# Equal tile sizes for the strided attention cells, and a new planner of the issue order

## The chip, the cores and the metric

The kernel runs on one core of a Trainium2 chip. A core has five engines that run their own instruction streams: TensorE (PE, matrix products; PEld is its weight load), VectorE (DVE), ScalarE (ACT), GpSimdE (POOL) and SyncE (SP, which here issues every DMA). Matmuls read SBUF and write PSUM, which has eight banks of 2 KB per partition. The metric is the device time of one execution, in microseconds.

## The reference

Three stages follow each other. Only the first has masks:

```python
scores = (1 / sqrt(64)) * q @ k.T               # 4 batches, 8 heads, 576 tokens, head size 64
mask_local   = (rel >= 0) & (rel < 32)           # heads 0..3, rel = query - key
mask_strided = (rel >= 0) & (key % 32 == query % 32)   # heads 4..7
attn = softmax(where(mask, scores, -1e9)); x = attn @ v          # x: 2304 tokens x 512
h = x @ w_in; solu = h * softmax(h)                              # 512 -> 1024
y = layernorm(solu) * g_ln @ w_out                               # 1024 -> 512
out = (y @ w_a * (y @ w_b)) @ w_out2                             # 512 -> 1536 -> 512
```

Weights arrive as 64-bit floats, and are rebuilt as 32-bit floats on the chip.

## The kernel before

**Attention.** A strided head has 32 residues of 18 tokens each, and tokens see only their own residue. The kernel puts three residues in a cell of 54 queries by 54 keys; a head's 16 residues of one parity make five such cells and one of a single residue, 18 by 18. A strided tile is one pair of heads and one parity j: 12 cells, of which ten are 54 wide and two are 18 wide. There are 16 strided tiles (4 batches, 2 pairs, 2 parities). A local cell has 64 queries and 96 keys; a local tile has eight cells (one tile in three has two), and there are 24.

For each tile PE runs two operations of the plan. `scores` (L705 to L710) first adds the mask to PSUM by a product of an identity in bf16 with a table of 0 and a large negative number (L706), and then adds q times k per cell (L709; fp32, each cell shows as two records in the trace). `pv` multiplies the transposed softmax with v: L803 in fp32 for batch 0, and L808, L809, L810 for the others, three fp16 products per cell that add up. `pv` of all tiles writes one PSUM bank, `xbank`, head 0 to partitions 0 to 63 and head 1 to 64 to 127. An operand of up to 32 rows or columns uses a 32-wide part of the PE array, one of 33 to 64 a 64-wide part.

**After attention.** `moe1` computes h (L861, 24 matmuls per 128 tokens), its softmax and layer norm on DVE, ACT and POOL, and transposes the result by DMA; `s2` computes y (L910). L910 needs all of w_out: eight raw pieces are loaded, rebuilt (ACT L468, DVE L470, L475, L481), measured (ACT L514), scaled, and split into two fp16 parts (ACT L546, DVE L548, eight times each). The last stage runs products of y with w_a and w_b (L1288) and then with w_out2 (L1353).

**The order.** Every operation goes through `Plan.op` with an engine, a cost in microseconds, and for PE a number of columns. `Plan.schedule` makes a forward list schedule by keys, a backward one that gives new keys, adds noise (a seeded random number), and repeats 120 times; the order with the shortest replay is emitted. The replay doubles the cost of a PE operation when the columns of the time window before it were below `ENTRY`; `forward` also prefers operations with many columns per microsecond (`dense`) when few columns were issued lately. So the order on all engines and DMA queues follows from the costs given to `Plan.op`. One instruction stream per engine runs in this order: an instruction that waits holds back all that stand behind it on its engine.

Of the kernel before, what the change touches and what calls it, by code (L numbers as in the profile page):

```python
# [25 lines left out]
ST = 32  # L26
# [7 lines left out]
NM = S // QT  # L34
# [16 lines left out]
NEG = -(2.0 ** 120)  # L51
PASSES = ((0, 0), (0, 1), (1, 0))

PARAM = dict(back=12, first=40, early=(0,), seed=4, noise=0.1, direct=(0,), span=4.0, dense=1500, cols=5000, pf1=(),
             pf2=(), ph1=(), pv=(), pp=(8,), ps1=(), ps2=(), passes=120, e=3,
             PT=3, raw=2, rawl=2, raws=2, qkT=2, V=2, wk=2, xt=1, ln=2, lnT=2, ys=2, raw64=3, f64f=4, att=100.0,
             win=24.5, wout=128.6, moff=-69.7, moe=96.6, conv2=257.2, dconv=15.0, p2=385.0, pre=6.5, fine=(),
             lat=1, plo=(0,), sooner=0.0, soon=(((0, 0), (0, 1), (1, 0), (1, 1)), ((0, 2), (0, 3), (1, 2), (1, 3), (2, 0), (2, 1), (2, 2), (2, 3)), ()), cv=-40.0, dcv=10.0)
# [37 lines left out]
class Plan:  # L96
# [3 lines left out]
    TICK, ENTRY = 10.24 / 3, 3060  # L100
    SAME = dict(DVE=0.13, ACT=0.15, POOL=0.05, PE=0.0, CTL=0.0)
    ENGINES = ("PE", "DVE", "ACT", "POOL", "SP", "CTL")

    def __init__(self):
        self.ops, self.writer, self.readers, self.key, self.sooner, self.shift = [], {}, {}, 0.0, 0.0, 0.0

    def op(self, eng, us, fn, r=(), w=(), nbytes=0, after=()):
        o = Op()
        o.eng, o.us, o.fn, o.key, o.nbytes, o.sooner = eng, us, fn, self.key - self.sooner, nbytes, self.sooner
        o.deps, o.starts, o.outs = set(after), set(), []  # L110
# [25 lines left out]
        o.deps.discard(o)  # L136
        self.ops.append(o)
        return o

    def latency(self, a, b):  # L140
        if a.eng == b.eng and a.eng != "SP":
            return self.SAME[a.eng]
        return PARAM["lat"] * (0.28 if a.eng == "PE" else 0.14)

    def schedule(self):

        order, self.shift = self.forward(), 0.0
        best, keys = self.length(order), [o.key for o in self.ops]  # L150
        rnd = random.Random(PARAM["seed"])
        for n in range(PARAM["passes"]):
            if n % PARAM["back"] == 0 and n >= PARAM["first"]:
                for o, key in zip(self.ops, keys):
                    o.key = key
                self.shift = shift
                self.forward()
            self.backward()
            for o in self.ops:
                o.key += rnd.gauss(0.0, PARAM["noise"]) - o.sooner  # L160
            self.shift = self.TICK * (n % 4) / 4
            order = self.forward()
            length = self.length(order)
            if length < best:
                best, keys, shift = length, [o.key for o in self.ops], self.shift
        for o, key in zip(self.ops, keys):
            o.key = key
        self.shift = shift
        order = self.forward()
        self.mean = best  # L170
        return order

    def length(self, order):
        return sum(self.replay(order, self.TICK * (n + 0.5) / 4) for n in range(4)) / 4

    def replay(self, order, shift):
        free = {e: 0.0 for e in self.ENGINES}
        dma = hw = 0.0
        count, start, end = collections.defaultdict(float), {}, {}
        for o in order:  # L180
            e = o.eng
            at = free[e]
            for d in o.deps:
                at = max(at, end[d] + self.latency(d, o))
            for d in o.starts:
                at = max(at, start[d])
            us = o.us
            if e == "PE":
                if count[int((at + shift) / self.TICK) - 1] < self.ENTRY:
                    us *= 2  # L190
                self.fill(count, at + shift, us, o.nbytes)
            start[o] = at
            free[e] = end[o] = at + us
            if e == "SP":
                hw = max(hw, at) + 0.55
                dma = max(dma, hw + 0.65) + o.nbytes / 250e3
                free[e] = max(free[e], hw, dma - 2.0)
                end[o] = dma + 0.75
        return max(end.values())

    def fill(self, count, t, us, cols):
        end = t + us
        while t < end:
            n = int(t / self.TICK)
            e = min(end, (n + 1) * self.TICK + 1e-4)
            count[n] += cols * (e - t) / us
            t = e

    def backward(self):
        for o in self.ops:  # L210
            o.n, o.ready = len(o.outs), 0.0
        free = {e: 0.0 for e in self.ENGINES}
        ready = {e: [o for o in self.ops if o.eng == e and not o.n] for e in self.ENGINES}
        dma = 0.0
        for _ in self.ops:
            at, e = min((max(free[e], min(o.ready for o in ready[e])), e) for e in self.ENGINES if ready[e])
            o = max((o for o in ready[e] if o.ready <= at), key=lambda o: (o.end, o.seq))
            ready[e].remove(o)
            end = free[e] = at + o.took
            if e == "SP":  # L220
# [4 lines left out]
            for d in o.deps:  # L225
                d.ready = max(d.ready, end + self.latency(d, o))
                d.n -= 1
                if not d.n:
                    ready[d.eng].append(d)
# [1223 lines left out]
```

## Time and profile before

| | |
|---|---|
| median of 3 runs | 740.57 us (739.69 to 744.24) |
| profiled execution: span | 742.1 us |
| PE busy | 719.9 us, 97% |
| DVE busy | 519.3 us, 70% |
| ACT busy | 432.2 us, 58% |
| POOL busy | 117.2 us, 16% |
| chain that ended last | 88% PE, 6% DVE, 2% ACT, 2% DMA |

The profiled execution's own time is not listed apart from the runs; its span of 742.1 us stands 1.5 us above their median. Busy PE time counts a matmul from its start to its modelled end, so matmuls that overlap count once, and a PE that is slow in issuing still counts as busy. The distance from one matmul's start to the next one's tells more than its length. The column PEclk is the share of PE's full clock that was granted: 1.00 is 2.4 GHz and 0.50 is 1.2 GHz.

### The profile page before, as it was taken

How to read it: one execution, taken by the hardware profiler on the slowest of the kernel's cores; microseconds unless marked ns; L12 is line 12 of the kernel's file. 1: busy time of each engine (PE TensorE's matmuls, PEld its weight loads, DVE VectorE, ACT ScalarE, POOL GpSimd, SP SyncE). 2: the span in 40 equal slices, each digit the busy share in tenths (PEclk: the TensorE clock that was granted, in tenths of full speed). 3: DMA queues.
4: the chain of work that ended last, by engine and by line, in shares of the span. 5: the costliest groups of instructions: out<-in, count | busy, mean ns of one | idle time of the engine just before them, and what ended most of it. 6: DMA issues, size and time to landing. Idle time of an engine off the chain costs nothing.

```text
span 742.1 us, 14124 instructions
## 1 busy us (share of the span) xinstructions
PE 719.9 (97%) x5444; PEld 479.2 (65%) x5444; DVE 519.3 (70%) x1020; ACT 432.2 (58%) x824; POOL 117.2 (16%) x194
## 2 busy tenths in 40 slices
PE   6989889999999999999999999999999999999997
PEld 4867668888787888878655555555555546555553
DVE  4888987858776864898899998547868454434252
ACT  4667977676777876785768666544454333132230
POOL 4441435412433432210000000000000000000000
PEclk9988979999999999999999999999999999999999
DMA  9788996976998585567537034406705031711304
GB/s 212 181 193 222 193 153 136 221 178 160 218 208 165 118 190 141 149 123 254 194 142 272 20 129 129 142 28 187 246 1 170 29 126 44 236 57 46 124 6 165
DMA packets 159327, 109.61 MB, mean 148 GB/s; under 512 B 103702, under 2 KB 137500, under 8 KB 159260
## 3 DMA queue, kind: packets, MB, share of 16 engines
q1 hardware_dynamic: 159260, 108.71, 56.6%
q8 instruction: 43, 0.70, 0.4%
q14 instruction: 24, 0.20, 0.1%
HBM read 65.42 MB, written 27.53 MB: 125 GB/s over the span
## 4 chain that ended last, share of the span: by engine, by line
PE 88%; DVE 6%; ACT 2%; DMA 2%; issue 1%; SPq 0%; POOL 0%; POOLq 0%; DVEq 0%
PE M L1288 31%; PE o L1353 19%; PE y L910 12%; PE h L861 12%; PE s L709 4%; PE s L624 3%; PE xbank L808 2%; PE xbank L803 1%; PE s L706 1%; DMA raw<-in_moe_w_b_dram 1%; PE xbank L810 1%; DMA rawk<-in_k_dram 1%; DMA rawq<-in_q_dram 1%; PE xbank L809 1%; ACT qkT L632 1%
## 5 line engine op out<-in xcount | busy, mean ns | idle before, releaser
L1288 PE MATMUL M<-y,w 128*128 128x384 f16 x1512 | 256.4, 326 | 0.9 <-DVE y L1235 0.6
L1288 PEld LDWEIGHTS <-w 128*128 128x128 f16 x1512 | 147.8, 98 | 102.5 <-issue 1.6
L1353 PE MATMUL o<-wo,p 128*128 128x512 f16 x648 | 147.9, 379 | 0.0
L1353 PEld LDWEIGHTS <-p 128*128 128x128 f16 x648 | 63.3, 98 | 71.0
L910 PE MATMUL y<-lnT,wout 128*128 128x256 f16 x864 | 105.0, 279 | 0.8 <-ACT ys L913 0.6
L910 PEld LDWEIGHTS <-wout 128*128 128x128 f16 x864 | 83.9, 100 | 15.4 <-issue 2.5
L861 PE MATMUL h<-win,xh 128*128 128x512 f32 x288 | 81.5, 422 | 1.4 <-DVE wk L869 1.3
L1295 ACT COPY M<-M 128x384 f32<-128x384 f32 x72 | 33.5, 466 | 68.3 <-PE M L1288 68.2
L861 PEld LDWEIGHTS h<-win,xh 128*128 128x128 f32 x288 | 55.1, 201 | 13.2 <-DVE wk L869 1.1
L1338 ACT ACTIVATE p<-A 128x384 f16<-128x384 f32 x72 | 36.7, 520 | 33.2 <-DVE A L1337 33.1
L1360 DVE SCALAR_TENSOR_TENSOR ob<-o,osc,op 128x512 f32<-128x512 f32 x36 | 27.0, 750 | 40.4 <-PE o L1353 35.1
L1340 DVE SCALAR_TENSOR_TENSOR p<-A,p 128x384 f16<-128x384 f32 x72 | 38.8, 552 | 8.0 <-ACT p L1338 7.7
L709 PE MATMUL s<-qkT 64*54 64x54 f32 (+2 forms) x672 | 38.4, 254 | 2.7 <-ACT qkT L632 2.4
L1299 DVE TENSOR_TENSOR A<-M,V 128x384 f32<-128x384 f32 x36 | 20.0, 555 | 30.0 <-PE M L1288 29.9
L475 DVE SCALAR_TENSOR_TENSOR f64f<-f64f,raw 128x512 int32<-128x512 int32 x52 | 39.4, 762 | 1.4 <-ACT f64f L468 0.7
L866 DVE TENSOR_REDUCE st<-h 128x1 f32<-128x1024 f32 x18 | 22.0, 1221 | 25.9 <-PE h L861 25.9
L861 PE MATMUL h<-win,xl 128*128 128x512 f32 x144 | 40.0, 400 | 0.0
L1337 DVE TENSOR_TENSOR A<-A,M 128x384 f32<-128x384 f32 x36 | 19.9, 552 | 27.0 <-PE M L1288 26.8
L468 ACT ACTIVATE f64f<-raw 128x512 f32<-128x512 f32 x52 | 34.5, 670 | 7.1 <-DMA raw<-in_moe_w_out_dram 2.9
L1310 ACT COPY V<-M 128x384 f32<-128x384 f32 x36 | 17.1, 475 | 34.4 <-PE M L1288 34.3
L709 PEld LDWEIGHTS s<-qkT 64*54 64x54 f32 (+2 forms) x672 | 27.7, 143 | 13.4 <-issue 3.6
L784 POOL TENSOR_TENSOR e<-e,r 128x324 f32<-128x324 f32 (+2 forms) x30 | 26.6, 889 | 59.5 <-DVE r L740 59.5
(170 smaller groups left out, 1135.7 us busy)
## 6 DMA issues: line engine op xcount, KB each, us to landing
raw<-in_moe_w_out_dram SPq DMA_DIRECT2D x20, 512.0 KB
o_scr<-ob SPq DMA_DIRECT2D x36, 256.0 KB
op<-o_scr SPq DMA_DIRECT2D x36, 256.0 KB
raw<-in_moe_w_a_dram SPq DMA_DIRECT2D x12, 512.0 KB
raw<-in_moe_w_b_dram SPq DMA_DIRECT2D x12, 512.0 KB
y_scr<-y SPq DMA_DIRECT2D x14, 384.0 KB
y<-y_scr SPq DMA_DIRECT2D x14, 384.0 KB
y_scr<-ys SPq DMA_DIRECT2D x18, 256.0 KB
```

The source lines that it names most:

```text
L468: act(0.67, lambda: nc.scalar.activation(f(), raw()[:, :, 1].bitcast(F32), AF.Copy, scale=2.0 ** -112), (raw,), (f,))
L475: nc.vector.scalar_tensor_tensor(fi, fi, 3, raw()[:, :, 0], op0=ALU.logical_shift_left, op1=ALU.bitwise_or)
L709: nc.tensor.matmul(s[64 * half:64 * half + nq, f, col:col + kk], g.T()[w, 0, q0:q0 + nq], g.T()[w, 1, k0:k0 + kk], start=False, stop=n == ...
L784: pool(0.1 + 1.2 * pl, lambda: nc.gpsimd.tensor_tensor(ev(), ev(), r()[:, :ng].unsqueeze(2).to_broadcast([128, ng, nk]), op=ALU.mult), (r, ...
L861: nc.tensor.matmul(h()[:, 512 * n:512 * n + 512], xs[xa]()[:, kk], win[wa][:, kk, 512 * n:512 * n + 512], start=(pi == 0 and kk == 0), sto ...
L910: nc.tensor.matmul(y()[:, 256 * mi:256 * mi + 256], wout[:, kk, wa, 128 * m:128 * m + 128], lnT()[:, xa, kk], start=(pi == 0 and kk == 0), ...
L1288: nc.tensor.matmul(bank()[:, :HB], w()[:, wa, a, kk], y7[b]()[:, xa, kk], start=first and pi == 0 and kk == 0, stop=pi == 2 and kk == 1, s ...
L1295: act(TA, lambda: nc.scalar.copy(dst()[:, :HB], src()[:, :HB]), (src,), (dst,))
L1338: act(TA, lambda x=x, v=v: nc.scalar.activation(v(0), x(), AF.Copy, scale=2.0 ** -PEXP), (x,), ((pu, 0, c, t),))
L1340: dve(TD, lambda x=x, v=v: nc.vector.scalar_tensor_tensor(v(1), x(), 2.0 ** -PEXP, v(0), op0=ALU.mult, op1=ALU.subtract), (x, (pu, 0, c, t ...
L1353: nc.tensor.matmul(o(), pus[u]()[:, xa, c, 128 * tt:128 * tt + 128], wo()[:, 2 * u + c, wa], start=(u == 0 and c == 0 and pi == 0), stop=( ...
L1360: dve(0.75, lambda: nc.vector.scalar_tensor_tensor(ob(), o(), osc()[:, tt:tt + 1], op(), op0=ALU.mult, op1=ALU.add), (o, osc, op), (ob,))
```

## The change

The kernel computes the same. Six things differ.

1. In `scores` a cell of 18 queries is computed with 36 (`LEAST`): 18 further rows of the output that nobody reads. It then needs a 64-wide part of the array, as the cells of 54 do.
2. The mask product is split: instead of one product with the whole array, one per 64 output partitions, in the same quarter of the array that the cells use.
3. In `pv` of strided tiles a cell of 18 keys is computed with 54; the further rows are zero. The cells are also taken in another order: head 0 and head 1 of the same block follow each other, where before the two halves of one head did.
4. The costs and column counts of PE operations are new. Columns are weighed by the share of the array that they use, and `scores` and `pv` have `mode` 1, all else 0.
5. `forward` picks among ready PE operations of both modes, staying in the mode of the last one for up to `stay` = 1.0 us of key, and adds `SWITCH` = 0.095 us where the mode changes; the `dense` rule is gone. The cost at the low clock is now followed through the operation (`matmuls`).
6. 200 rounds instead of 120; three phases of the clock instead of four in the mean.

```diff
-    TICK, ENTRY = 10.24 / 3, 3060
+    TICK, ENTRY, SWITCH = 10.24 / 3, 2710, 0.095
...
+    def matmuls(self, count, t, us, cols):
+
+        tick, per = self.TICK, cols / us if us else 0.0
+        while True:
+            w = int(t / tick)
+            rate = 1.0 if w and count[w - 1] >= self.ENTRY else 0.5
+            room = (w + 1) * tick - t
+            if us <= room * rate:
+                count[w] += per * us
+                return t + us / rate
+            count[w] += per * room * rate
+            us -= room * rate
+            t = (w + 1) * tick + 1e-9
...
+            a = able[e]
+            if e == PE and able[6]:
+                b = able[6]
+                if not a or b[0][0] + (0.0 if was else PARAM["stay"]) < a[0][0] + (PARAM["stay"] if was else 0.0):
+                    a = b
+            i = pop(a)[1]
+            start[i] = at
+            if e == PE:
+                x = us[i] if mode[i] == was else us[i] + self.SWITCH
+                was = mode[i]
+                stop = free[e] = self.matmuls(count, at + shift, x, cols[i]) - shift
...
-            for m, off in ((maskl[rows, :1], ST * half), (maskl[rows, 1:], ST)):
+            for m, off in ((maskl[rows, :1], 0), (maskl[rows, 1:], ST)):
...
-                for rows, stop in ([(slice(0, 128), False)] if len(last) == 2 * len(banks) else
-                                   [(slice(64 * x, 64 * x + 64), (f, x) not in last) for x in range(2)]):
-                    nc.tensor.matmul(s[rows, f, :npb * nk], identb[:, rows], mask[:, :npb], start=True, stop=stop)
+                for x in range(2):
+                    rows = slice(64 * x, 64 * x + 64)
+                    w = slice(64 * f, 64 * f + 64)
+                    nc.tensor.matmul(s[rows, f, :npb * nk], identb[w, w], masked[x][w, :npb], start=True,
+                                     stop=(f, x) not in last)
+            qk = g.T().rearrange("p c s -> p (c s)")
             for n, (h, f, col, half, _, nq, q0, kk, k0, *_) in enumerate(cells):
-                w = slice(64 * f, 64 * f + 64)
-                nc.tensor.matmul(s[64 * half:64 * half + nq, f, col:col + kk], g.T()[w, 0, q0:q0 + nq],
+                w, nq = slice(64 * f, 64 * f + 64), max(nq, LEAST)
+                nc.tensor.matmul(s[64 * half:64 * half + nq, f, col:col + kk], qk[w, q0:q0 + nq],
                                  g.T()[w, 1, k0:k0 + kk], start=False, stop=n == last[f, half])
-        pe(ng * nk * 0.42e-3 + sum(0.04 if c[3] else 4 * c[7] / 2.4e3 for c in cells) + 0.03, scores,
+        groups = [c[7] for c in cells if not c[3] and (g.strided or not c[0])]
+        pe(ng * nk * 0.42e-3 + sum(4 * kk / 2.4e3 + 0.01 for kk in groups) + 0.03, scores,
...
+        turns = sorted(cells, key=lambda c: (-c[9], c[3], c[0])) if g.strided else cells
...
-            for h, f, _, half, rb, nq, q0, kk, _, blk, p0, vc in cells:
+            for h, f, _, half, rb, nq, q0, _, _, blk, p0, vc in turns:
+                kk = nk
```

Where the instructions stand, at three places. On PE, the second operation of the program: the scores of the first strided tile, before and then after (s is the score tile in PSUM, masks the table, identb the identity, qkT the transposed q and k).

```order
L624 MATMUL s<-ident,rawk 128x96 x6
L706 LDWEIGHTS identb
L706 MATMUL s<-masks,identb 128x324
L709 MATMUL s<-qkT 54x54
L709 MATMUL s<-qkT 18x18
L709 MATMUL s<-qkT 54x54
L709 MATMUL s<-qkT 18x18
L709 MATMUL s<-qkT 54x54 x8
```

```order
L666 MATMUL s<-ident,rawk 128x96 x6
L749 LDWEIGHTS identb
L749 MATMUL s<-masks,identb 64x324
L749 LDWEIGHTS identb
L749 MATMUL s<-masks,identb 64x324
L754 MATMUL s<-qkT 54x54
L754 MATMUL s<-qkT 36x18
L754 MATMUL s<-qkT 54x54
L754 MATMUL s<-qkT 36x18
L754 MATMUL s<-qkT 54x54 x8
```

The 18-row cells have 36 rows now, and the mask is two products of 64 rows.

On PE, the first fp16 `pv` of a strided tile, from the last product of its first cell on (V is v's high or low part, PT the transposed softmax).

```order
L810 MATMUL xbank<-PT,V_1285 64x54
L808 LDWEIGHTS V_1275
L808 MATMUL xbank<-PT,V_1275 64x18
L809 LDWEIGHTS V_1275
L809 MATMUL xbank<-PT,V_1275 64x18
L810 LDWEIGHTS V_1285
L810 MATMUL xbank<-PT,V_1285 64x18
L808 LDWEIGHTS V_1275
L808 MATMUL xbank<-PT,V_1275 64x54
```

```order
L858 MATMUL xbank<-PT,V_1264 64x54
L856 LDWEIGHTS V_1241
L856 MATMUL xbank<-PT,V_1241 64x54
L857 LDWEIGHTS V_1241
L857 MATMUL xbank<-PT,V_1241 64x54
L858 LDWEIGHTS V_1264
L858 MATMUL xbank<-PT,V_1264 64x54
L856 LDWEIGHTS V_1241
L856 MATMUL xbank<-PT,V_1241 64x18
```

Behind the first cell there was the 18-wide cell of the same head; now there is the 54-wide cell of the other head.

On ACT, the last three of the eight splits of w_out that L910 waits for, before and then after (raw is a weight piece that a DMA has just brought, f64f its rebuilt form).

```order
L889 ACTIVATE ln<-wk,st 128x1024
L546 ACTIVATE wout<-wout,gs_sb 128x512
L830 ACTIVATE xT<-xbank,sc 128x16x18
L734 ACTIVATE e<-e 128x384
L468 ACTIVATE f64f<-raw_1056 128x512
L468 ACTIVATE f64f<-raw_1261 128x512
L546 ACTIVATE wout<-wout,gs_sb 128x512
L830 ACTIVATE xT<-xbank,sc 128x16x18
L739 ACTIVATE sm_1421<-sm_1421 128x4
L734 ACTIVATE e<-e 128x384
L546 ACTIVATE wout<-wout,gs_sb 128x512
```

```order
L510 ACTIVATE f64f<-raw_1116 128x512
L588 ACTIVATE wout<-wout,gs_sb 128x512
L878 ACTIVATE xT<-xbank,sc 128x16x18
L922 ACTIVATE ln,st<-wk 128x1024
L588 ACTIVATE wout<-wout,gs_sb 128x512
L780 ACTIVATE e<-e 128x384
L878 ACTIVATE xT<-xbank,sc 128x16x18
L780 ACTIVATE e<-e 128x384
L588 ACTIVATE wout<-wout,gs_sb 128x512
```

Two of the three rebuildings of w_a and w_b that stood ahead of the last split now stand behind it. Up to the first L910, PE has the same work in both programs: eight strided and eight full local score tiles, h for four tiles of 128 tokens, and three fp16 `pv` of strided tiles.

## Rows read from the trace of the kernel before

**Rows 1.** the page's first lines: span; busy us, share of the span, instructions.

```profile
span 742.1 us, 14124 instructions
...
PE 719.9 (97%) x5444; PEld 479.2 (65%) x5444; DVE 519.3 (70%) x1020; ACT 432.2 (58%) x824; POOL 117.2 (16%) x194
```

**Rows 2.** stretches: us; busy PE, PEld, DVE, ACT, POOL; PEclk, DMA share, GB/s.

```profile
0.00:50.00 50.00, 40.65 (x389) 32.54 (x390) 35.13 (x68) 27.77 (x53) 21.88 (x40) 0.97 0.86 191
50.00:100.00 50.00, 46.14 (x354) 34.98 (x354) 45.66 (x89) 42.85 (x86) 18.97 (x27) 0.86 0.93 196
```

**Rows 3.** stretches between changes of the granted clock, same columns.

```profile
104.59:114.83 10.24, 7.98 (x74) 5.84 (x70) 9.01 (x19) 7.21 (x14) 3.94 (x6) 0.50 0.52 91
114.83:166.03 51.20, 51.20 (x566) 42.03 (x565) 34.83 (x66) 37.15 (x67) 19.36 (x29) 1.00 0.88 184
166.03:169.45 3.42, 3.42 (x13) 2.82 (x12) 3.15 (x11) 2.18 (x5) 0.15 (x1) 0.50 0.46 141
169.45:230.89 61.44, 60.73 (x701) 48.89 (x700) 45.15 (x84) 45.95 (x90) 22.18 (x38) 1.00 0.95 200
230.89:234.30 3.41, 3.41 (x18) 2.43 (x17) 3.41 (x7) 0.69 (x2) 1.54 (x3) 0.50 0.61 187
...
286.00:345.00 59.00, 58.24 (x446) 48.30 (x444) 48.86 (x87) 43.10 (x67) 9.24 (x20) 1.00 0.63 166
345.00:400.00 55.00, 54.08 (x328) 31.84 (x326) 50.84 (x107) 38.94 (x74) 0.00 (x0) 1.00 0.53 180
```

**Rows 4.** timeline of PE, one strided score tile: start us, us, what.

```profile
215.28 0.30 PE L706 MATMUL s<-masks,identb 128*128 128x324 bf16 x1
215.52 1.36 PE L709 MATMUL s<-qkT 64*54 64x54 f32 x24
216.81 1.05 PE L910 MATMUL y<-lnT,wout 128*128 128x256 f16 x8
```

**Rows 5.** stretches of L709 alone in that tile: us; busy PE, PEld; PEclk, DMA.

```profile
215.51:216.26 0.75, 0.74 (x8) 0.57 (x8) 1.00 0.75 232
216.26:216.81 0.55, 0.55 (x18) 0.48 (x16) 1.00 1.62 134
```

**Rows 6.** timeline of PE, one fp16 `pv` of a strided tile.

```profile
100.61 0.21 PE L808 MATMUL xbank<-PT,V 54*64 54x54 f16 x1
...
100.81 0.19 PE L808 MATMUL xbank<-PT,V 18*64 18x18 f16 x1
...
101.39 0.21 PE L808 MATMUL xbank<-PT,V 54*64 54x54 f16 x1
...
101.48 0.21 PE L808 MATMUL xbank<-PT,V 54*64 54x54 f16 x2
...
101.59 0.19 PE L808 MATMUL xbank<-PT,V 54*64 54x54 f16 x2
...
101.78 0.19 PE L808 MATMUL xbank<-PT,V 54*64 54x54 f16 x1
...
101.97 0.34 PE L706 MATMUL s<-maskl,identb 128*128 128x192 bf16 x2
```

**Rows 7.** timeline of PE, one local score tile.

```profile
192.69 0.34 PE L706 MATMUL s<-maskl,identb 128*128 128x192 bf16 x2
192.96 0.56 PE L709 MATMUL s<-qkT 64*64 64x96 f32 x16
```

**Rows 8.** timelines of DVE, ACT and PE around the first L910.

```profile
74.97 1.23 DVE L866 TENSOR_REDUCE st<-h 128x1 f32<-128x1024 f32 x1 [3.09 <-PE h L861]
...
105.89 0.66 ACT L468 ACTIVATE f64f<-raw 128x512 f32<-128x512 f32 x1 [1.88 <-DMA raw<-in_moe_w_b_dram]
...
109.06 0.74 DVE L548 SCALAR_TENSOR_TENSOR wout<-wout,gs_sb 128x512 f16<-128x512 f32 x1
...
110.36 4.96 PE L910 MATMUL y<-lnT,wout 128*128 128x256 f16 x24
...
116.61 2.79 PE L910 MATMUL y<-lnT,wout 128*128 128x256 f16 x24
```

More of the change, by code (lines that the diff above doesn't have):

```diff
@@ L1 @@
-import collections
+import heapq
 import random
@@ L142, in latency @@
             return self.SAME[a.eng]
-        return PARAM["lat"] * (0.28 if a.eng == "PE" else 0.14)
+        return 0.28 if a.eng == "PE" else 0.14
     def schedule(self):
-        order, self.shift = self.forward(), 0.0
-        best, keys = self.length(order), [o.key for o in self.ops]
-        rnd = random.Random(PARAM["seed"])
[L152 to L162, printed above, removed]
-            length = self.length(order)
-            if length < best:
-                best, keys, shift = length, [o.key for o in self.ops], self.shift
@@ L166, in schedule @@
[L166 to L170, printed above, removed]
-        return order
[L173 to L207, printed above, removed]
-    def backward(self):
[L210 to L213, printed above, removed]
-        dma = 0.0
[L215 to L220, printed above, removed]
-                dma = max(at + 0.75, dma) + o.nbytes / 250e3
-                end = dma + 1.2
-                free[e] = max(free[e], dma - 2.0)
-            o.key = self.span - end
[L225 to L229, printed above, removed]
-            for d in o.starts:
-                d.n -= 1
-                if not d.n:
-                    ready[d.eng].append(d)
@@ new lines, in schedule @@
+        key, shift = [o.key for o in ops], 0.0
+        order = self.forward(key, shift)
+        self.mean = self.length(order)
+        best = order, key, shift
+        rnd = random.Random(PARAM["seed"])
+        for t in range(PARAM["passes"]):
+            if t % PARAM["back"] == 0 and t >= PARAM["first"]:
+                self.forward(best[1], best[2])
+            key = [k + rnd.gauss(0.0, PARAM["noise"]) for k in self.backward()]
+            shift = self.TICK * (t % 4) / 4
+            order = self.forward(key, shift)
+            length = self.length(order)
+            if length < self.mean:
+                self.mean, best = length, (order, key, shift)
@@ new lines, in schedule, with length @@
+        return [ops[i] for i in best[0]]
+    def length(self, order):
+        return sum(self.replay(order, self.TICK * (k + 0.5) / 3) for k in range(3)) / 3
+    def matmuls(self, count, t, us, cols):
[10 more added lines that the diff above has]
+            t = (w + 1) * tick + 1e-9
@@ L692, in att_tile @@
         npb = ng // len(banks)
-        mask = masks if g.strided else maskl[:, 1:] if j else maskl
+        masked = [masks] * 2 if g.strided else [maskl[:, 1:] if j or x else maskl for x in range(2)]
         sp = rings["s"].new()
@@ L776, in att_tile @@
                 (r, *ee), (tok,))
-            pe(nblk * 0.11, transposes, (tok, "ident"), (pt,), nblk * 128)
+            pe(nblk * 0.11, transposes, (tok, "ident"), (pt,), nblk * rows * 2)
             def evac():
```

208 lines of the change are left out of this document (143 added, 65 removed).

## The prediction, made before the changed kernel was run

> **What bounds the kernel now.** I read the page first. PE is busy for 719.9 of the span's 742.1 us, DVE for 519.3 [rows 1]: in the mean PE is the bound, and what PE is spared should come off the end. The mean hides a first part that is different, so I read the stretches next. In the first 50 us PE is busy for 40.65 us and in the next 50 for 46.14, while DVE there has 35.13 and 45.66 [rows 2]. From 114.83 us on PE has no idle time in 51.20 us, and 0.71 us in the 61.44 us that follow the short stretch behind them [rows 3]. What separates the two parts is the first y product, L910. It starts at 110.36, and the last of the eight splits of w_out on DVE starts at 109.06 and takes 0.74 us [rows 8]. I call this point the gate. Before it PE has only attention and h, both fed by DVE and ACT; behind it y gives PE work at any moment.
>
> So the time is the gate plus what PE has to do behind it, and a microsecond of PE is worth a microsecond only behind the gate. Last I read PE's timeline of single tiles, by the distance from one start to the next. In a strided score tile the first four cells take 0.75 us and the other eight 0.55 [rows 5]. In a strided `pv` the first cell and the switch to the 18-wide one take 0.20 us (100.61 to 100.81), four such cells 0.78 (to 101.39); behind them a lone cell takes 0.09 (to 101.48) and a pair of two 54-wide cells 0.10 to 0.11 (101.48 to 101.59) [rows 6]. The expensive thing is the change between 54 and 18, not the arithmetic.
>
> **The change, part by part.**
>
> *Scores of strided tiles.* One tile takes 1.53 us, 215.28 to 216.81 [rows 4]. The eight equal cells take 0.55 us with the way out to the next operation. For that way I take 0.12 us, as a `pv` needs from its last product on (below), so a pair costs (0.55 - 0.12) / 4 = 0.11. With the padding the first four cells become two such pairs, 0.22 for 0.75: 0.53 us less. The 18 further rows of output cost nothing, since the products' columns stay 18. The bounds are 0, if the stall had another cause than the width, and 0.64, if a pair costs the 0.055 us of half a pair.
>
> *Its mask.* From the mask's start to the first cell there are 0.24 us [rows 4]. Two products of a quarter array each run side by side as the cells do, and the change to small tiles moves ahead of them. I cost it at nothing; the bounds are +0.14 (the two masks run one after the other) and -0.10 (the way in is hidden by an operation in the same mode ahead of it).
>
> *Masks of local tiles.* Two full products come before the cells, 0.27 us [rows 7]. One of 324 columns and the way in take 0.24 [rows 4], two of 192 take 0.27: 60 columns are 0.03 us, so 192 are about 0.09. Four quarter products at once take one such time instead of two: 0.09 us less, with 0 and 0.18 as bounds.
>
> *`pv` of strided tiles.* One takes 1.36 us, 100.61 to 101.97, and the last product is at 101.85, as its cell starts at 101.78 and has three products: 0.12 us for the way out [rows 6]. With one width and head 0 next to head 1, twelve cells are six pairs: 6 x 0.105 + 0.12 = 0.75, so 0.61 us less. The padding from 18 to 54 keys adds rows to the array, not columns. The Trainium skill (TensorEngine Tiling (Array Packing), PSUM Pressure) says that different row tiles cannot access the same PSUM bank at the same time; the new neighbours are just that, rows 0 to 63 and 64 to 127 into xbank. The trace disagrees: the pairs at 101.48 and 101.59 are of different heads, write xbank, and cost 0.105 together where one alone costs 0.09 [rows 6]. By that rule the twelve cells would take 12 x 0.09 + 0.12 = 1.20, and 0.16 us would be spared instead of 0.61.
>
> *How many behind the gate.* The order puts eight strided score tiles and three strided `pv` ahead of the first L910 in both programs. Of 16 and 12 (fp16), eight scores, nine `pv` and 13 local score tiles lie behind it: 8 x 0.53 + 9 x 0.61 + 13 x 0.09 = 4.2 + 5.5 + 1.2 = **10.9 us**.
>
> *The gate.* PE is spared as much again ahead of it, the fp32 `pv` of batch 0 included, but this counts only as far as DVE and ACT get the splits out earlier. DVE idles 14.87 + 4.34 = 19.2 us in the first 100 [rows 2], which is the most. Two waits go by the new order. ACT waited 1.88 us for a piece of w_b in front of the last two splits [rows 8]; that rebuilding now stands behind them. DVE waited 3.09 us for h [rows 8], and PE was late there with strided score tiles just ahead of it. These are **5.0 us**; the bounds are 0 and 10, half of DVE's idle time. What is late next is DVE's own row of instructions, which has the same work up to the last split but for one reduction of h.
>
> *The clock.* Behind the gate PE ran at 1.2 GHz (granted 0.50) in 104.59 to 114.83, of which 4.5 us count, and in 3.42 and 3.41 us later [rows 3]. 24 y products took 4.96 us in the first of these and 2.79 at 2.4 GHz [rows 8], so half of the time is lost: 5.7 us. Each followed strided tiles or idle time. Strided tiles are shorter now, but two of their score tiles still stand in a row at two places. I take half, **2.8 us**; the bounds are 5.7 and -3.4, two more such stretches.
>
> *New waits.* The order of everything is new. From 286 to 400 us DVE has 48.86 of 59 and 50.84 of 55 us, and PE idles 0.76 + 0.92 = 1.7 there [rows 3]. An attention stage that ends earlier asks DVE for the last stage's operands earlier. I add as much idle time again, **1.7 us**; the cover is DVE's slack of 16.4 + 16.3 us in 114.83 to 166.03 and 169.45 to 230.89 [rows 3], without which the last rival below applies.
>
> The sum: 742.1 - 10.9 - 5.0 - 2.8 + 1.7 = 725.1. The span stands 1.5 us above the median of the runs, so I predict **723.6 us**.
>
> **The rivals.**
>
> - *The transfers bound the attention stage.* The DMA engines are busy for 0.95 of the 61.44 us from 169.45 on and 0.88 of the 51.20 before [rows 3]. If 0.95 is as much as they do, the longer stretch cannot shrink, and half of the 10.9 and the two later clock gains (1.7) are lost: 723.6 + 5.4 + 1.7 = 731. Against it: PE waited for no transfer there.
> - *The rule on row tiles holds* and paired cells of two heads run one after the other: 9 x 0.45 = 4.1 us less gain, 728. The pairs in [rows 6] speak against it. It is the rule of the Trainium skill named above.
> - *The padding does not remove the stall* (the change does not do what it says), since it comes from the new operand and not from its width: the scores' 4.2 us and most of `pv`'s 5.5 stay, 731 to 733. Against it, the eight equal cells also change operands, at a fifth of the price.
> - *More is gained ahead of the gate*: the gate comes 10 us earlier, and the clock does not fall behind it: 723.6 - 5.0 - 2.9 = 716.
> - *Slower: raw weights block the queues.* In the new order SP issues two pieces of w_a and w_b right ahead of two transposes of the softmax. SP and ACT work in order, and ACT has shown 1.88 us of waiting for one such piece [rows 8]. If each of the 12 early pieces now costs that on PE's path, 22.6 us come on: 746. From 17/12 = 1.4 us per piece on, the change would not pay. DMA shares up to 0.95 speak for it; that ACT waited so only once near the gate speaks against it.
> - *DVE bounds the start of the last stage* after all: then the 99.7 us of DVE work in 286 to 400 cannot follow PE, and of the 17 us only some 14 can be had: 727. It lies in the forecast's range.
>
> **How the numbers follow.** Chances: the forecast with its bounds 0.65, transfers 0.13, row tiles 0.05, no effect of the padding 0.05, more ahead of the gate 0.08, blocked queues 0.04. Taking each term's worst likely value alone, the forecast's case reaches from 717 (the gate at its bound) to 731 (gate at 0, a half of the clock gain lost). The range goes to **714** on one side, with both the gate and the clock at their good ends (716) and the masks' ways in hidden, and to **736** on the other, the transfers' 731 with the gate at 0.
>
> A measurement of this kernel cannot tell less than about 1% from no change, that is 733.2 to 748.0. Faster by more: nearly all of the forecast, the row tiles and the early gate, and most of the transfers and of the padding's case, 0.86. Within: 0.11. Slower by more: 0.03, the blocked queues at a higher price than one wait.
>
> **What would show it.** Right: a strided score tile of 0.95 to 1.05 us and a strided `pv` of 0.7 to 0.8 from start to next start; 18-column cells that follow 54-column ones without the 0.1 us gap; four local mask products that start within 0.05 us; the first L910 (now L958) at 103 to 107 us; PE without idle time from there to 286. Wrong: `pv` cells of two heads 0.09 us apart (row tiles); PE idle in front of `pv` with a DMA as releaser (transfers, or blocked queues); the first L910 at 110 or later; more stretches at granted 0.50 behind it than two; PE waits for DVE between 290 and 380. A time over 736 would say that the plan as a whole went wrong, not one of the cells.

## The result, and the profile after

The changed kernel takes **719.51 us** (median; 718.48 to 723.23 in 5 runs) where the kernel before takes 740.57: a ratio of 0.9723, 95% interval 0.9693 to 0.9753, 2.8% faster. 723.6 was predicted, with 714 to 736 as the range. The profiled execution has a span of 721.5 us, against 742.1; with what lies around the span it took 723.23, the longest of the five. The medians here and below leave out one execution of 842.81 us at a mean granted clock of 0.80, of the new cells in the old order run again.

The page's first lines, as in [rows 1]:

```profile
span 721.5 us, 14209 instructions
...
PE 690.6 (96%) x5492; PEld 459.4 (64%) x5492; DVE 518.0 (72%) x1020; ACT 429.7 (60%) x824; POOL 121.2 (17%) x194
```

PE lost 29.3 us of busy time, the span 20.6. DVE and ACT have the same work but for 1.3 and 2.5 us.

The tiles, on PE's timeline: a strided score tile (answers to [rows 4]), a strided `pv` (to [rows 6]) and a local score tile (to [rows 7]).

```profile
113.06 0.33 PE L749 MATMUL s<-masks,identb 64*64 64x324 bf16 x2
113.22 0.76 PE L754 MATMUL s<-qkT 64*54 64x54 f32 x24
113.91 0.27 PE L564 MATMUL xbank<-ident,am 128*2 128x128 f32 x1
...
210.26 0.22 PE L856 MATMUL xbank<-PT,V 54*64 54x54 f16 x2
...
210.38 0.18 PE L856 MATMUL xbank<-PT,V 54*64 54x18 f16 x2
...
210.48 0.20 PE L856 MATMUL xbank<-PT,V 54*64 54x54 f16 x2
...
210.76 0.20 PE L856 MATMUL xbank<-PT,V 54*64 54x54 f16 x2
...
210.95 0.38 PE L666 MATMUL s<-ident,rawk 96*128 96x96 f32 x2
...
207.49 0.28 PE L749 MATMUL s<-maskl,identb 64*64 64x192 bf16 x4
207.59 0.50 PE L754 MATMUL s<-qkT 64*64 64x96 f32 x16
208.03 0.23 PE L856 MATMUL xbank<-PT,V 96*64 96x64 f16 x2
```

From start to next start the strided score tile has gone from 1.53 to 0.85 us, the strided `pv` from 1.36 to 0.69. The "x2" of a `pv` row is two cells of two heads that start together; the next pair follows 0.09 to 0.12 us later, the 18-column pair at 210.38 included. The four masks of a local tile start together, and the first cell follows 0.10 us later, where it was 0.27.

The gate, on DVE's and PE's timelines (answers to [rows 8]):

```profile
97.94 0.73 DVE L590 SCALAR_TENSOR_TENSOR wout<-wout,gs_sb 128x512 f16<-128x512 f32 x1
...
98.50 0.39 PE L958 MATMUL y<-lnT,wout 128*128 128x256 f16 x2
```

L958 is the former L910. It starts 11.9 us earlier than at 110.36, and the last split of w_out on DVE stands beside it again. But that split does not release it: the split ends at 98.67, when the first y product is already under way. The first eight y products read only the high parts of w_out, which ACT writes; the low parts of DVE come in with the ninth, 0.9 us later. In both kernels the first y product follows PE's product ahead of it without idle time. So the gate is where PE's own row of instructions reaches y, and what holds that row up ahead of it is looked for below.

The first 100 us (answer to [rows 2]) and the stretches between changes of the clock (to [rows 3]), with the same columns:

```profile
0.00:50.00 50.00, 37.25 (x432) 29.76 (x433) 41.10 (x84) 32.63 (x65) 28.84 (x44) 0.90 0.92 218
...
98.50:213.28 114.78, 114.05 (x1485) 95.32 (x1488) 95.20 (x187) 95.77 (x184) 47.40 (x73) 1.00 1.03 208
213.28:216.70 3.42, 3.42 (x47) 2.52 (x36) 3.32 (x11) 3.30 (x9) 2.08 (x5) 0.50 1.06 218
216.70:274.73 58.03, 55.08 (x534) 44.97 (x531) 38.72 (x67) 41.31 (x79) 20.35 (x36) 1.00 0.70 152
274.73:281.55 6.82, 5.97 (x16) 4.57 (x15) 6.75 (x15) 4.08 (x6) 2.22 (x3) 0.50 0.91 306
281.55:345.00 63.45, 62.12 (x459) 47.58 (x458) 52.23 (x101) 44.65 (x74) 6.26 (x11) 1.00 0.60 177
345.00:400.00 55.00, 52.10 (x298) 28.89 (x296) 51.42 (x105) 41.02 (x76) 0.00 (x0) 1.00 0.42 147
```

DVE works 41.10 of the first 50 us, where it had 35.13. Behind the gate PE has 0.73 us idle in 114.78; then it waits, 2.95, 0.85, 1.33 and 2.90 us in the four stretches from 216.70 to 400. The view of PE's waits behind the gate names many small ones:

```profile
PE o L1399 <- DVE p L1386: 1.6, 1, 1.6
PE o L1399 <- ACT ob L1409: 1.3, 1, 1.3
PE h L909 <- DVE wk L917: 1.3, 2, 0.8
PE h L909 <- DVE xl L902: 1.0, 1, 1.0
PE xbank L856 <- ACT xT L878: 0.9, 3, 0.4
PE y L958 <- DVE small L979: 0.9, 1, 0.9
```

(Columns: us in total, how often, the longest.)

### The profile page after: what moved, and what is told of

The parts are those of the page before. It is cut to its first block, busy times and chain, and to the rows that moved or that the text cites. A ratio compares the mean times of both kernels' runs of the same rounds, so it can differ in the third digit from the quotient of the medians.

```text
span 721.5 us, 14209 instructions
## 1 busy us (share of the span) xinstructions
PE 690.6 (96%) x5492; PEld 459.4 (64%) x5492; DVE 518.0 (72%) x1020; ACT 429.7 (60%) x824; POOL 121.2 (17%) x194
## 4 chain that ended last, share of the span: by engine, by line
PE 89%; DVE 6%; ACT 2%; issue 2%; DMA 1%; POOL 0%; SPq 0%; DVEq 0%; ACTq 0%; POOLq 0%
PE M L1334 34%; PE o L1399 19%; PE h L909 15%; PE y L958 12%; PE s L666 3%; PE s L754 2%; PE xbank L856 1%; PE s L749 1%; DVE wk L917 1%; DVE f64f L517 1%; DMA rawk<-in_k_dram 1%; PE xbank L858 1%; DVE st L914 1%; PE xbank L857 1%; DVE raw L512 0%
## 5 line engine op out<-in xcount | busy, mean ns | idle before, releaser
L1399 PE MATMUL o<-wo,p 128*128 128x512 f16 x648 | 148.6, 379 | 2.9 <-DVE p L1386 1.6
L1399 PEld LDWEIGHTS <-p 128*128 128x128 f16 x648 | 63.2, 98 | 73.7 <-DVE p L1386 2.1
L958 PE MATMUL y<-lnT,wout 128*128 128x256 f16 x864 | 102.0, 275 | 1.8 <-DVE small L979 0.9
L958 PEld LDWEIGHTS <-wout 128*128 128x128 f16 x864 | 83.0, 99 | 15.7 <-issue 4.8
L517 DVE SCALAR_TENSOR_TENSOR f64f<-f64f,raw 128x512 int32<-128x512 int32 x52 | 36.4, 707 | 0.7
L838 POOL TENSOR_TENSOR P<-e,P 128x324 f16<-128x324 f32 (+2 forms) x30 | 30.6, 1030 | 13.8 <-ACT P L837 13.7
L909 PEld LDWEIGHTS h<-win,xl 128*128 128x128 f32 x144 | 27.7, 196 | 7.4 <-DVE xl L902 1.5
L1345 DVE TENSOR_TENSOR C<-M,V 128x384 f32<-128x384 f32 x36 | 20.0, 554 | 14.1 <-PE M L1334 14.0
```

The source lines that it names most:

```text
L517: nc.vector.scalar_tensor_tensor(fi, fi, 3, raw()[:, :, 0], op0=ALU.logical_shift_left, op1=ALU.bitwise_or)
L838: pool(0.15 + 1.4 * pl, lambda: nc.gpsimd.tensor_tensor(plo, ev(), ph, op=ALU.subtract), (e, ("P2", pi, 0)), (("P2", pi, 1),))
L909: nc.tensor.matmul(h()[:, 512 * n:512 * n + 512], xs[xa]()[:, kk], win[wa][:, kk, 512 * n:512 * n + 512], start=(pi == 0 and kk == 0), sto ...
L958: nc.tensor.matmul(y()[:, 256 * mi:256 * mi + 256], wout[:, kk, wa, 128 * m:128 * m + 128], lnT()[:, xa, kk], start=(pi == 0 and kk == 0), ...
L1345: dve(TD, lambda: nc.vector.tensor_tensor(t(), x()[:, :HB], c4(), op=ALU.add), (x, *r4), (t,))
L1399: nc.tensor.matmul(o(), pus[u]()[:, xa, c, 128 * tt:128 * tt + 128], wo()[:, 2 * u + c, wa], start=(u == 0 and c == 0 and pi == 0), stop=( ...
```

## The experiments

Three theories went on record with the first runs: (A) the cheaper cells make the gain, by what PE is spared behind the gate, and little of what it is spared ahead of it counts; (B) PE bounds from the start, and what it is spared counts in full everywhere; (C) the new order makes most of the gain.

### Cells and order taken apart

**The new cells in the order of before.** Planner, costs and keys are those of before; only what a tile emits is new.

```diff
+LEAST = 36
...
+                w, nq = slice(64 * f, 64 * f + 64), max(nq, LEAST)
...
+        turns = sorted(cells, key=lambda c: (-c[9], c[3], c[0])) if g.strided else cells
...
+                kk = nk
```

> The new cells (padding, quarter masks, head 0 next to head 1) in the order of before: the planner, its costs and so every queue's order are those of before. By the changed kernel's trace a strided score tile takes 0.85 us where it took 1.53, a strided pv 0.69 where it took 1.36, a full local score tile 0.54 where it took 0.76. Theory A (PE time counts only behind the first L910): 8 x 0.68 + 9 x 0.67 + 13 x 0.2 = 14 us behind the gate, and 0 to 5 us from an earlier gate: 722 to 727 us. Theory B (PE bounds from the start, so what is spared ahead of the gate counts in full, some 13 us more): about 713. Theory C (the new order makes most of the gain, not the cells): 733 or more.

Measured: 720.81 us, ratio 0.9746 (0.970 to 0.9792). The whole gain is there without the new planner, within what the intervals can tell: B and C fall. A comes nearest and is 1 us off its range, since the gate gave 7.9 us (below) where it had 0 to 5.

**The old cells in the new order**: the changed kernel with the edits of the cells reversed.

> The order of the changed kernel on all engines and queues, with the cells, masks and pv of before. Theory A: the first L910 comes earlier by the waits of ACT and DVE that the order removes, some 5 us, and PE does the old work behind it: 733 to 738. Theory C: 725 or less. If the order fits only the short cells, waits come on: 740 or more.

Measured: 747.18 us, ratio 1.0102 (1.007 to 1.0134). The new order alone makes the kernel 1% slower, although its gate is earlier (108.47 for 110.36). A's 733 to 738 missed; the last case came true, an order that fits only the short cells. The two parts in the stretches ahead of the gate and behind it (columns as in [rows 2]); the kernel before, the changed one, the new cells in the old order, the old cells in the new order:

```profile
0.00:110.36 110.36, 94.49 (x881) 73.42 (x881) 89.08 (x175) 77.97 (x152) 42.48 (x69) 0.90 0.89 194
110.36:742.10 631.74, 625.43 (x4566) 405.74 (x4564) 430.23 (x846) 354.19 (x672) 74.73 (x126) 0.99 0.51 140
```

```profile
0.00:98.50 98.50, 80.34 (x904) 62.37 (x905) 84.13 (x170) 75.12 (x147) 42.88 (x67) 0.88 0.93 205
98.50:721.50 623.00, 610.24 (x4589) 397.05 (x4588) 433.92 (x851) 354.59 (x678) 78.32 (x127) 0.99 0.54 144
```

```profile
0.00:102.45 102.45, 79.87 (x905) 62.96 (x905) 88.46 (x172) 77.61 (x152) 42.10 (x68) 0.95 0.94 208
102.45:717.80 615.35, 607.82 (x4592) 393.93 (x4588) 433.53 (x849) 353.12 (x673) 73.48 (x126) 1.00 0.52 143
```

```profile
0.00:108.47 108.47, 96.35 (x881) 73.44 (x881) 84.49 (x174) 75.34 (x149) 42.37 (x68) 0.95 0.87 188
108.47:745.00 636.53, 624.87 (x4565) 406.30 (x4564) 431.83 (x847) 353.99 (x675) 78.36 (x127) 0.99 0.51 140
```

Read the DVE column ahead of the gate. With the old order DVE has the same work there with either cells, 89.08 and 88.46 us, but idles 110.36 - 89.08 = 21.3 us with the old and 14.0 with the new: the cells take 7.3 us of waiting from it, and the gate comes 7.9 earlier. The new order has only 84.13 and 84.49 us of DVE work ahead of its gate: it puts some 4.3 us of it behind. Its gate comes 4.0 us earlier than with the old order where the cells are new (98.50 for 102.45), and 1.9 earlier where they are old. Behind the gate PE idles 12.8 and 11.7 us with the new order, 7.5 and 6.3 with the old. Its longest waits there are the same with either cells (1.6 us for DVE and 1.3 for ACT at the line that is L1399 in the changed kernel), so they come with the order. That they are the price of the DVE work put behind the gate is likely, but no run shows it.

Which of DVE's waits the cells shortened shows in the view of its waits ahead of the gate, before and then with the new cells in the old order:

```profile
DVE mx L722 <- PE s L709: 5.5, 4, 4.2
DVE st L866 <- PE h L861: 3.6, 2, 3.1
```

```profile
DVE mx L726 <- PE s L713: 3.1, 1, 3.1
...
DVE st L872 <- PE h L867: 1.3, 1, 1.3
```

Both are waits for PE, 9.1 us and then 4.4: 4.7 of the 7.3 us. ACT's wait for a piece of w_b is still there (1.78 us for 1.88), and it lies on the way to the gate in both kernels: PE's last `pv` ahead of y stands behind a product (L537, then L538) that waits for ACT, and ACT's row waits for the piece. SP issues the piece 8.05 us earlier with the new cells, and the gate comes 7.9 earlier with it. SP's, ACT's and PE's rows, before and then with the new cells in the old order (ACT's row of before is in [rows 8]):

```profile
100.34 0.50 SPq L460 DMA_DIRECT2D raw<-in_moe_w_b_dram  x1
...
107.86 0.58 PE L537 MATMUL xbank<-row,ones 1*128 1x2 f32 x2 [1.44 <-ACT sm L739]
```

```profile
92.29 0.53 SPq L461 DMA_DIRECT2D raw<-in_moe_w_b_dram  x1
...
98.86 0.66 ACT L469 ACTIVATE f64f<-raw 128x512 f32<-128x512 f32 x1 [1.78 <-DMA raw<-in_moe_w_b_dram]
...
100.83 0.58 PE L538 MATMUL xbank<-row,ones 1*128 1x2 f32 x2 [2.47 <-ACT sm L743]
```

With the new order ACT has no such wait near the gate. The chain of work that ended last tells the same of the whole stretch ahead of the gate; here are its pieces up to the gate, summed by engine:

| cells, order | gate, us | PE busy up to it | chain on PE | chain on DVE |
|---|---|---|---|---|
| old, before | 110.36 | 94.49 | 55.4 | 18.7 |
| new, old order | 102.45 | 79.87 | 13.3 | 53.7 |
| old, new order | 108.47 | 96.35 | 89.6 | 2.2 |
| new, new order | 98.50 | 80.34 | 56.3 | 20.4 |

With the old order the new cells take PE off the chain and DVE takes its place, so only 7.9 of the 14.6 us that PE is spared ahead of the gate come through. With the new order PE stays the largest part of the chain with either cells, and 10.0 of 16.0 come through. (The chain is the profile's inference, and differs between executions: another one of the changed kernel has 45.4 and 17.7.)

**The new strided cells in half of the batches**, 0 and 1 or 2 and 3 (order and local masks of before).

```diff
+            new = g.strided and g.b in (0, 1)
...
+                kk = nk if g.strided and g.b in (0, 1) else kk
```

> As c1_cells_old_order, but only strided tiles of batches 0 and 1 have the new cells: eight scores, four fp32 pv and three of four fp16 pv, all ahead of the first L910 in this order. About 8 x 0.7 + 4 x 1.1 + 3 x 0.67 = 12 us of PE are spared there, and one pv (0.7 us) behind. Theory A: 735 to 740, as far as the first L910 comes earlier. Theory B: about 728. Theory C: 738 or more.

> As c1_cells_old_order, but only strided tiles of batches 2 and 3 have the new cells: eight scores and eight pv, all behind the first L910. 8 x 0.68 + 8 x 0.67 = 10.8 us. Theories A and B: 728 to 731, more by up to 3 if the two later stretches at the low clock go too. Theory C, or transfers that bound the attention stage: 735 or more.

Measured: 735.22 us (ratio 0.9936, 0.9913 to 0.996) and 730.03 (0.9872, 0.9819 to 0.9925): 4.4 and 9.6 us gained. Batches 0 and 1 stand ahead of the gate but for one `pv`, batches 2 and 3 behind it. About 12 us of PE ahead of the gate are worth 4.4 (its gate comes at 105.46, 4.9 earlier), and 10.8 behind it are worth 9.6. Both times lie in A's ranges, and neither in C's; B missed the first by 7 us. Theory A stands, for the old order.

### The parts of the cells

Each kernel has the new cells in the old order, with one edit undone. The new cells complete have 720.8 us (and 720.4 when run again, below).

**Score widths undone.**

```diff
-LEAST = 36
+LEAST = 1
```

> The new cells in the order of before, but with the first four score cells of a strided tile back at their own widths (54, 54, 18, 18) in place of 54 everywhere; masks and pv stay new. If the change of width is what cost time (my theory): a strided score tile goes from 0.85 to about 1.38 us, since the four cells took 0.75 before and two pairs take 0.22. Eight such tiles stand behind the first y product, 8 x 0.53 = 4.2 us, and eight ahead of it, of which some 2 us count by what the gate gave for the cells (7.9 us for 12): from 720.8 to about 727. If it was the new operand and the mask's way in, not the width (rival): the tile stays at 0.85 to 0.95 and the time at 721 to 722.

(The complete new cells are padded to 36, not to 54, and the widths undone are 54, 18, 54, 18 in sequence.)

**`pv` widths undone**, the heads next to each other as in the change.

```diff
-            for h, f, _, half, rb, nq, q0, _, _, blk, p0, vc in turns:
-                kk = nk
+            for h, f, _, half, rb, nq, q0, kk, _, blk, p0, vc in turns:
```

> The new cells in the order of before, but the pv cells of a strided tile keep their own widths (54 or 18 keys); the new order of the cells (heads next to each other) stays. If only the change of width costs (about 0.10 us each) and the new order already puts cells of one width side by side: two changes are left where there were four, 0.2 us a tile, nine tiles behind the gate: 1.8 us, and some 0.5 ahead of it, about 723. If each 18-wide cell costs a way in and out of its own: 0.4 us a tile and 725. If the padding is worth nothing beside the order of the heads: 721.

**`pv` sequence undone**, all cells padded as in the change.

```diff
-        turns = sorted(cells, key=lambda c: (-c[9], c[3], c[0])) if g.strided else cells
+        turns = cells
```

> The new cells in the order of before, but the pv cells of a strided tile are issued in their old sequence (padded to 54 keys throughout). If two cells of different heads side by side is what gives the pairs of 0.095 us and lone cells cost 0.09 each, the cells that lose their neighbour cost as much as a pair: up to four more such steps, 0.1 to 0.4 us a tile, 1 to 4 us behind the gate, 722 to 725. If the equal width is all that counts: 721, with a pv of 0.69 us as now.

**Masks as full products again.**

```diff
-                for x in range(2):
-                    rows = slice(64 * x, 64 * x + 64)
...
+                for rows, stop in ([(slice(0, 128), False)] if len(last) == 2 * len(banks) else
```

> The new cells in the order of before, but the mask products go back to full-array form: one product of 128 rows per bank in place of two or four quarter ones. If the quarter masks spare what the trace shows (0.08 to 0.10 us ahead of a strided tile's cells, 0.22 us in a local tile: 0.76 before, 0.54 now): 8 x 0.09 + 13 x 0.2 = 3.3 us behind the gate and some 1 us ahead: about 725. If that saving in the local tile comes from what follows it and not from the masks: 721 to 722.

| undone | time, us | ratio (95%) | the tile, us from start to next | full change | gate | PE's work behind it |
|---|---|---|---|---|---|---|
| score widths | 726.12 | 0.9813 (0.979, 0.9835) | strided score 1.41 | 0.85 | 102.88 | 610.6 |
| `pv` widths | 723.32 | 0.9772 (0.9748, 0.9796) | strided `pv` 0.91 | 0.69 | 104.97 | 608.4 |
| `pv` sequence | 722.71 | 0.9764 (0.9742, 0.9785) | strided `pv` 0.77 | 0.69 | 102.87 | 607.0 |
| masks | 727.13 | 0.9817 (0.9792, 0.9842) | strided score 0.97, local score 0.76 | 0.85, 0.54 | 104.01 | 609.3 |

(PE's work behind the gate is the stretch from there to the end, less PE's idle time in it and half of its time at 1.2 GHz. The new cells complete have a gate of 102.45 and 606.4 us of work.)

PE's timeline of a strided score tile with the widths undone, and of a `pv` with its widths undone:

```profile
202.65 0.33 PE L708 MATMUL s<-masks,identb 64*64 64x324 bf16 x2
202.81 1.31 PE L713 MATMUL s<-qkT 64*54 64x54 f32 x24
204.06 1.05 PE L916 MATMUL y<-lnT,wout 128*128 128x256 f16 x8
```

```profile
223.87 0.22 PE L813 MATMUL xbank<-PT,V 54*64 54x54 f16 x2
...
224.08 0.20 PE L813 MATMUL xbank<-PT,V 18*64 18x18 f16 x2
...
224.28 0.22 PE L813 MATMUL xbank<-PT,V 54*64 54x54 f16 x2
224.33 0.20 PE L814 MATMUL xbank<-PT,V 54*64 54x54 f16 x2
...
224.40 0.20 PE L813 MATMUL xbank<-PT,V 54*64 54x54 f16 x2
```

The four score cells with their own widths cost 0.56 us more. In `pv` the pair of 18-key cells starts 0.21 us after the pair ahead of it and holds the next one off for 0.20, where pairs of one width follow at 0.12: 0.22 us in a tile for two changes of width, **0.11 us a change** between these fp16 cells. The Trainium skill (TensorEngine Tiling (Array Packing), Key Properties) says that a change of the tiling mode drains TensorE; the trace fits that, and gives the change this price; that the change from 54 to 18 is one of mode is inferred from the sizes. In `pv` the two edits are not a sum: either alone takes most of the 0.67 us, the padding 0.59 (1.36 to 0.77) and the sequence 0.45 (1.36 to 0.91), since each also takes away most of the changes.

The differences in time are 5.3, 2.5, 1.9 and 6.3 us from 720.8. Behind the gate the tiles give 8 x 0.56 = 4.5; 9 x 0.22 = 2.0; 9 x 0.08 = 0.7; and 8 x 0.12 + 8 x 0.22 + 5 x 0.17 = 3.6, and the traces agree: PE's work there grows by 4.2, 2.0, 0.6 and 2.9 us from 606.4. What the times have beyond that, 0.5 to 2.7 us, goes with a later gate (0.4, 2.5, 0.4 and 1.6 us), idle time and the clock, and is not taken apart further. The theories by which widths or masks are worth nothing have fallen. Of the two `pv` edits the times alone show neither, since their intervals overlap that of the complete cells; the tiles (0.91 and 0.77 for 0.69) and the work behind the gate show them.

### What an order is worth

Four kernels on one chip: the changed kernel, the new cells in the old order, and two other orders of the new cells.

> The changed kernel as it is, beside the next three on one chip. If its order is worth nothing on these cells (my theory), it stands within 0.3% of the new cells in the order of before, at a ratio of 0.972 to 0.976 to the kernel before. If the 4 us that its first y product comes earlier are worth something at the end, it is 2 us or more faster than that kernel.

> The new cells in the order of before, once more, on the same chip as the changed kernel. Both theories as there: 719.5 to 721 us and equal to the changed kernel, or 2 us and more slower than it.

The old planner, with the changed kernel's costs for the tiles:

```diff
-        pe(ng * nk * 0.42e-3 + sum(0.04 if c[3] else 4 * c[7] / 2.4e3 for c in cells) + 0.03, scores,
+        pe(ng * nk * 0.42e-3 + sum(4 * kk / 2.4e3 + 0.01 for kk in groups) + 0.03, scores,
```

> The new cells, planned by the planner of before (its rules untouched) with the changed kernel's costs for the score and pv tiles. The order of before was made for cells that cost more, so if an order made for these costs is what the new planner contributes, this one should reach the changed kernel or pass it: 716 to 720 us. If one order of these cells is as good as another (my theory): 719 to 722, with the first y product at 98 to 103 us and what it gains given back behind it as idle time of PE or at the low clock.

The new planner with `seed=7` for `seed=4`:

> The changed kernel with another seed of the planner's noise (7 for 4), which by the planner's own replay gives a program 3.7 us shorter. If its replay sees what limits the chip: 715 to 717 us, the fastest so far. If the replay misses it (my theory: the clock's short stretches and PE's waits of 0.4 to 1.6 us behind the gate fall where they fall): 718 to 723, no more to do with 3.7 us than with 0.

| cells, order | time, us | ratio (95%) | gate | behind it | PE idle there | at 1.2 GHz there | rest |
|---|---|---|---|---|---|---|---|
| old, before | 740.10 | 1 | 110.4 | 631.7 | 6.3 | 11.3 | 619.8 |
| old, new planner | 747.18 | 1.0102 | 108.5 | 636.5 | 11.7 | 10.2 | 619.7 |
| new, new planner (the change) | 720.01 | 0.9717 (0.9688, 0.9746) | 98.5 | 623.0 | 12.8 | 10.2 | 605.1 |
| new, old order | 720.41 | 0.9733 (0.9702, 0.9764) | 102.5 | 615.4 | 7.5 | 2.8 | 606.4 |
| new, old planner, new costs | 728.06 | 0.9843 (0.9813, 0.9873) | 104.5 | 625.0 | 11.6 | 13.4 | 606.7 |
| new, new planner, seed 7 | 722.26 | 0.9755 (0.9726, 0.9783) | 102.0 | 619.9 | 10.6 | 6.8 | 605.9 |

(Traces of the first run of each; the time of the old cells in the new order is that of the section above, from another chip. PE idle: the stretch behind the gate less PE's busy time in it, with some 4.0 us behind PE's last product in each. Rest: the stretch less the idle time and half of the time at 1.2 GHz.)

The last column settles the accounts. Behind the gate PE's own work is 619.7 to 619.8 us with the old cells and 605.1 to 606.7 with the new, in whatever order: the cells are worth 13 to 15 us there. Nearly all that an order does is in the gate, the idle time and the clock. For the changed kernel against the old order these are -4.0, +5.3 and +3.7: its earlier gate is spent. (The two profiles differ by 3.7 us the other way than the medians, since that of the change is of one of its longer executions and that of the old order of one of its shorter. The profile of the kernel before is of its longest too, so that the old cells' two spans differ by 2.9 us where the medians differ by 7.5. An account of an order by these traces is thus good to some 4 us, and the clock's share is the least certain. The last column agrees between such traces, 619.8 and 619.7.) On one chip the two differ by 0.4 us, with intervals that overlap. My theory that any order is as good fell with the third kernel: the old planner, given the new costs, made an order that is 8 us slower than the change, by a gate 6.0 later, 1.6 from 3.2 us more at half clock and 1.6 in the rest, less 1.2 of idle time. And the seed that was 3.7 us better by the planner's own replay came out 2.2 us slower, with intervals that overlap. So orders of these cells span at least 8 us, and in this case the replay saw a gain that did not come. Whether the new planner's rules avoid such an order or its seed was lucky stays open: each setting was run with one or two orders. No order beat the change, and the old order cannot be told from it.

## Why the prediction was right, and where it was not

The sum was 742.1 - 17.0 for the span; it came to 721.5, 20.6 less. The two traces compare well here: both are of the longest execution, 3.7 us over the median. Term by term:

- **PE behind the gate: -10.9 predicted, -14.7 measured** (619.8 to 605.1). The mechanism was right, each size too small. A strided score tile lost 0.68 us, not 0.53: two tiles in a row even come at 1.42 us together, and the mask, costed at nothing, gave 0.08 (0.24 to 0.16 from its start to the first cell). A `pv` lost 0.67, not 0.61. The local masks were the worst: 0.22 a tile for 0.09, outside its bounds of 0 to 0.18, most of it because the way from the masks to the first cell is 0.17 us shorter (0.27 to 0.10), and not only by half of the products' columns. Of the 13 local tiles behind the gate eight are full and five have two cells and gave 0.17: 8 x 0.75 + 9 x 0.67 + 8 x 0.22 + 5 x 0.17 = 6.0 + 6.0 + 2.6 = 14.6, with 0.75 as the mean over single tiles and pairs.
- **The gate: -5.0 predicted with 0 to -10 as bounds, -11.9 measured.** This step failed in its cause as well as its size, and the measured value lies outside its bounds. I took it from two waits, put both down to the new order, and let PE's shorter tiles count for nothing beyond them. The runs show 7.9 of it with the order untouched: PE was the largest part of the chain ahead of the gate (55.4 us), and faster tiles took it down to 13.3 and shortened DVE's waits for scores and h. The wait of ACT for w_b, 1.88 of my 5.0 us, was on the way to the gate, but it did not go with the cells (1.78); it is gone only in the new order. That order adds 4.0 us, or 1.9 with the old cells. How much of this is the wait for w_b and how much the DVE work put behind the gate, which my sum had as no cost, no run separates. The reading of the gate as the end of DVE's last split was wrong as well: PE's own row reaches y, and the split ends beside it.
- **The clock: -2.8 predicted, -0.5 measured** (half of 11.3 - 10.2). PE no longer ran at 1.2 GHz right behind the gate, but did in 213.28 to 216.70, behind the 114.78 us with only 0.73 of idle time, and in 274.73 to 281.55, behind 2.95 us of it. In the trace of the old order with the new cells this term is -4.3.
- **New waits: +1.7 predicted, +6.5 measured** (6.3 to 12.8). The place was half right: at L1399 PE waits 1.6 us for DVE and 1.3 for ACT, but 3.6 us fall in 243 to 276, among attention's last tiles, where I expected PE without idle time.

-14.7 - 11.9 - 0.5 + 6.5 = -20.6. The span was 3.6 us shorter than forecast: the gate and the cells came out 10.7 larger, and the waits and the clock took 7.1 of that back. The time was 4.1 off, since the span stood 2.0 us over the median and not 1.5. So the mechanism behind the gate was right, but that the time lay this near is in part luck: most of a miss of 10.7 us was cancelled by one of 7.1. Of the signs named, the `pv` of 0.69 us and the masks that start together came, but the score tile (0.85 for 0.95 to 1.05), the gate (98.50 for 103 to 107) and a PE without idle time up to 286 did not.

The rivals: transfers did not bind, with a DMA share of 1.03 over the 114.78 us behind the gate PE idled 0.73. The rule on row tiles fell, pairs of two heads into `xbank` follow at 0.10. That padding would not remove the stall fell with the undone widths. Weights did not block the queues: no wait for a raw piece is among PE's. "More is gained ahead of the gate" came true in its first half (a gate 11.9 earlier, no fall of the clock right behind it), and was given back later. DVE as the bound of the last stage shows as 1.6 us, not as 3.

## What to carry to other kernels

In this kernel, equal tile shapes in PE's quarters were worth more than what smaller unequal ones save: pad small cells to the size class of their neighbours (36 beside 54 was enough in the scores), and give masks the same shape as the cells. Price a microsecond of PE by where it falls: behind the gate nearly all of it counted, ahead of it about half, since there another engine took over the chain. When an expected release has passed already, follow the chain back to find what held the row up. When an order changes as well, compare cells and order apart, and add up gate, idle time and clock before crediting the planner.

## What was not expected of the hardware

The new cells with the `pv` sequence undone have the same order as the new cells complete, yet PE was granted a mean of 0.84 up to the gate, for 0.95, with 20.5 us at 1.2 GHz from 29.4 on (PE was busy for 15.82 us of them, and for 17.36 of the 20.5 that follow at full clock); these two stretches, and the one up to the gate:

```profile
29.40:49.90 20.50, 15.82 (x160) 11.88 (x160) 18.97 (x33) 14.65 (x31) 9.56 (x8) 0.50 0.93 216
49.90:70.40 20.50, 17.36 (x208) 13.76 (x206) 20.03 (x39) 17.74 (x36) 4.25 (x7) 1.00 0.91 219
...
0.00:102.87 102.87, 79.43 (x904) 62.47 (x905) 88.66 (x172) 77.69 (x152) 42.04 (x68) 0.84 0.93 208
```

The gate is at 102.87 there and at 102.45 in the other: with this order and these cells, where DVE has most of the chain ahead of the gate, even the clock hardly counted. The kernel with the score widths undone had such a stretch as well (31.67 to 52.15), and its gate is at 102.88.
